# Attention products in column tiles of 32, with x written in its final layout

## The chip, the cores and the metric

The kernel runs on one core of one Trainium2 chip. The metric is the device time of one execution, in microseconds (us); the number quoted for a kernel is the median of its runs. The engines are named as in the profile: PE (TensorE, with its weight loads shown apart as PEld), DVE (VectorE), ACT (ScalarE), POOL (GpSimd), and SP, whose queue issues every transfer (DMA) of this kernel.

## The reference

A gated linear attention with a complex state is followed by a two-layer network with a GELU:

```python
scale = np.minimum(mag, 0.999) / (mag + 1e-06)          # mag = |a_re + i a_im|
for t in range(S):                                       # S = 768
    new_re = ar * S_re - ai * S_im                       # (B, H, D, D) = (4, 8, 48, 48)
    new_im = ar * S_im + ai * S_re
    S_re, S_im = new_re + k[t] v[t]^T, new_im
    y[t] = q[t] . S_re
x = y as (B * S, H * D) = (3072, 384)
out = gelu(x @ w_in) @ w_out                             # w_in 384 x 2048, w_out 2048 x 384
```

The inputs of the attention are float32, the two weight matrices float64.

## The kernel before, in words

**Lanes.** The recurrence over t is turned into a chunked form. The sequence of 768 steps is cut in four groups (GROUPS, line 29: two chunks of 64, two of 64, two of 128, two of 128 steps). For each group, "lanes" of 128 partitions normalise `a`, run a complex running product (`scan`, lines 641 to 654) and multiply k and q by it. A group takes 4, 4, 8 and 8 slices; the last DVE step of a slice writes `xt` (line 631), and three transfers carry it to a scratch tensor `kq` in HBM (lines 633 to 635). This part is nearly all DVE and ACT work.

**Weights.** Each of 32 pieces of 128 x 384 float64 numbers is loaded into one of `N_RAW` buffers `raw`, taken apart by four DVE steps, one ACT copy and three PE products, and kept as a sum of two float32r parts, high and low (`weights`, lines 480 to 506). A buffer can be loaded anew once DVE, ACT and PE have read it.

**Units.** 24 units of 128 rows (one batch, 128 steps) do the attention proper (`unit`, from line 757): load `kqn` from `kq`; transpose k and q of each head on PE into `kT` and `qT`; multiply them to scores (lines 855 to 864); multiply the masked scores, still called `kT` and held in the buffers `kp`, with v into `py` (lines 866 to 873); add the old state `st` times q (`y_state`, lines 875 to 880); and turn and update the state (`turn_by_pe` or `turn_state`, then `add_state`, lines 822 to 839). Units 0 to 3 need the first lane group, units 4 to 7 the second.

In `py`, head h lies in the half h % 2 (64 rows, of which 48 are used) of piece h // 2. So there are four pieces of 96 useful rows, where the network wants three pieces of 128 rows, `xt[:, :, c]`. Pieces 0 to 2 are copied (twice: high part, then low part) straight into `xt`, piece 3 into a helper `x67`, and six transfers of 16 rows each move its rows into the gaps of `xt` (lines 914 to 931). The host lays the rows of w_in out to match (`w_pieces`, lines 222 to 227).

**Blocks.** Nine blocks of two or three units (BLOCKS, line 39) do the network: 16 groups f of 128 columns, for each nine (float32r) products into `ph`, two GELUs on ACT, a subtraction on DVE (`gl`), then nine products into `po` (lines 939 to 983).

**The order.** Every instruction is first noted in a plan; a list scheduler with a table of costs (lines 69 to 98) then chooses engine and order once, when the program is built. On the chip each engine's queue runs in that order and waits where something is late. `MORE` and `BIAS` are numbers that weigh the kinds of work.

All instructions of the plan carry line 398, so rows of the profile are told apart by their tiles: `tile written <- tiles read`.

Of the kernel before, what the change touches and what calls it, by code (L numbers as in the profile page):

```python
# [21 lines left out]
D2 = 2 * D  # L22
# [31 lines left out]
flag_w = flag_x + 2 * NU  # L54
# [28 lines left out]
ENTER, LEAVE = dict(narrow=0.093), dict(narrow=0.1)  # L83
# [8 lines left out]
EARLIER, N_RAW, N_KP = 1, 4, 2  # L92
# [4 lines left out]
MORE = dict(lanes0=70.56, lanes1=16.18, lanes2=-95.71, lanes3=149.81, weights0=-9.95, weights1=-62.12, units0=87.26, units1=95.47, units2=86.78, blocks0=48.05, blocks1=47.29, blocks2=56.39, checks=40.00)  # L97
BIAS = dict(vector=0.45, scalar=-0.52, gpsimd=0.35)
# [11 lines left out]
class Plan:  # L110
# [51 lines left out]
    def add(self, calls):  # L162
# [4 lines left out]
        for call in calls:  # L167
            outs, ins = self.operands(call)
            cost += self.cost(call, outs, ins)
            if engine == "tensor":  # L170
                step.form = ("turn" if call[1] == "transpose" else "round" if call[3]["rhs"].dtype == F32R else
                             "narrow" if call[3]["lhsT"].shape[1] <= 64 else "full")
# [24 lines left out]
    def cost(self, call, outs, ins):  # L197
# [6 lines left out]
        if engine == "tensor":  # L204
# [5 lines left out]

            if cols <= 64:
                return max(0.056, 2 * n * PASS)
# [196 lines left out]
def lanes_and_chunks(ctx, tc, flags, a_lanes, x_lanes, v_units, w_in, w_out, out):  # L409
# [318 lines left out]
    x67s = ring("x67", [128, 2, 128], 1, F32R)  # L728
# [23 lines left out]
    st = [cst.tile([D2, H, D], F32, name=f"st{b}", tag=f"st{b}")[:] for b in range(B)]  # L752
# [4 lines left out]
    def unit(u):  # L757
# [37 lines left out]
        def turn_state(i, b):  # L795

            sb = st[b]
# [9 lines left out]
        def turn_by_pe(i, b):  # L807
# [3 lines left out]
            P.vector.tensor_tensor(out=m2.rearrange("p c (h e) -> p c h e", h=H), in0=vap(sb, [[0, 2], [D, H], [1, D]]),  # L811
# [6 lines left out]
            sf = sb.rearrange("p h e -> p (h e)")  # L818
# [3 lines left out]
        def add_state(chunk, turned):  # L822

            i, _, _, t0, size, b = chunk
            sf = st[b].rearrange("p h e -> p (h e)")
            p = bank()[:, 0:DM] if turned is None else turned
            ps = p[0:D2]
# [37 lines left out]

        def y(some, halves=(0, 1)):

            with P.together():
                for hh in halves:
                    for h in range(hh * 4, hh * 4 + 4):  # L870
                        P.tensor.matmul(out=py[h % 2 * 64:h % 2 * 64 + 64, h // 2], lhsT=vn[:, h], rhs=kT[hh][:, h % 4], start=h < 2,
                                        stop=h > 5 and not with_state)
                y_state(some, halves)

        def y_state(some, halves=(0, 1)):
            for i, _, _, t0, size, b in some:
                for hh in halves:
                    for h in range(hh * 4, hh * 4 + 4):
                        P.tensor.matmul(out=py[h % 2 * 64:h % 2 * 64 + D, h // 2, t0:t0 + size], lhsT=st[b][:, h],
                                        rhs=qT[hh][0:D2, h % 4, t0:t0 + size], start=False, stop=h > 5 and i == with_state[-1][0])  # L880

        if early:
# [5 lines left out]
            py = held[0].rearrange("p (c l) -> p c l", c=4)  # L888
# [7 lines left out]
        else:  # L896
# [4 lines left out]
            py = held[0].rearrange("p (c l) -> p c l", c=4)  # L901
# [12 lines left out]
        xt, x67 = xblk[j][:, u - first_unit[j]], next(x67s)  # L914
        fc = flag_x + 2 * u
        parts = ((py[:, 3], x67[:, 0], x67[:, 1], fc), (py[:, 0:3], xt[:, :, 0], xt[:, :, 1], fc + 1))
        for at, hi, _, f in parts:
            P.scalar.activation(hi, at, AF.Copy, accum_out=flags[:, f:f + 1])
        if u < XPE:
            with P.together():  # L920
                for at, hi, _, _ in parts:
                    P.tensor.matmul(out=at, lhsT=minus[:], rhs=hi, start=False, stop=True, skip_group_check=True)
        for at, hi, lo, _ in parts:
            if u < XPE:
# [329 lines left out]
```

## Time and profile before

| | us |
|---|---|
| median of 3 runs (lowest, highest) | 700.38 (700.11, 700.49) |
| the profiled execution | 697.49 |
| its span, from first to last instruction | 695.8 |
| PE busy | 648.3 |
| DVE busy, ACT busy | 453.6, 465.4 |

The profile is of one execution. "Busy" is the time in which at least one instruction of an engine is under way, and products overlap in it, so a busy PE can still be slow. The granted clock is the share of the full TensorE clock (2.4 GHz) that the chip allowed; 0.5 is the lower level, 1.2 GHz. A float32 product shows as two records, a float32r product as one.

### The profile page before, as it was taken

To read this page: it belongs to the slowest core of one execution; us is meant where nothing else is said; L and a number is where in the kernel's file an instruction comes from. 1 tells how busy PE (TensorE), PEld (TensorE's weight loads), DVE (VectorE), ACT (ScalarE), POOL (GpSimd) and SP (SyncE) were. 2 spreads that over 40 slices of the span, in tenths; PEclk is the share of its full clock that TensorE was granted. 3 is DMA by queue.
4 is the path that set the end of the run, shared out by engine and by line. 5 is a ranking of instruction groups with operands and counts; after the bars stand their busy time and mean duration, and the time that the engine had idled before them with its cause. 6 is when DMAs were issued, how large, how long until landed. Compare 5 with 4: busy or idle time off the path is not lost.

```text
span 695.8 us, 14682 instructions
## 1 busy us (share of the span) xinstructions
PE 648.3 (93%) x5554; PEld 577.4 (83%) x5554; DVE 453.6 (65%) x1135; ACT 465.4 (67%) x1133; POOL 21.7 (3%) x61
## 2 busy tenths in 40 slices
PE   4486897998999999999999999999999999999996
PEld 2142576887899899888999999999999999999995
DVE  7999996997999999999999951244322212112221
ACT  6566676986989988986897764547563653555532
POOL 1001000030000000102000000000000000000000
PEclk9667998999999999999999999999999999999998
DMA  9378775585565557775764654334332523241200
GB/s 280 89 211 237 217 221 173 150 225 180 133 188 128 136 132 193 189 178 155 215 177 116 163 138 134 109 111 124 126 109 75 165 75 93 88 131 47 74 1 27
DMA packets 117325, 99.33 MB, mean 143 GB/s; under 512 B 56192, under 2 KB 105472, under 8 KB 117248
## 3 DMA queue, kind: packets, MB, share of 16 engines
q1 hardware_dynamic: 117248, 98.33, 50.5%
q8 instruction: 45, 0.74, 0.5%
q14 instruction: 32, 0.26, 0.1%
HBM read 69.40 MB, written 23.59 MB: 134 GB/s over the span
## 4 chain that ended last, share of the span: by engine, by line
PE 75%; ACT 8%; DMA 7%; DVE 6%; issue 1%; SPq 1%; ACTq 0%
PE po L398 28%; PE ph L398 26%; PE att L398 20%; DMA kqn<-kq 3%; ACT a L398 2%; DMA kq<-xt 2%; DVE a L398 2%; ACT tab L398 1%; SPq L398 1%; DMA a<-in_w_pieces_dram 1%; DVE tt L398 1%; ACT L396 1%; DVE xt L398 1%; ACT L398 1%; DVE bt L398 1%
## 5 line engine op out<-in xcount | busy, mean ns | idle before, releaser
L398 PE MATMUL ph<-xT,wi_hi 128*128 128x384 f32 (+1 forms) x864 | 209.7, 324 | 3.1 <-DMA xT<-x 3.1
L398 DVE TENSOR_TENSOR gl<-gf,gh 128x384 fp32r<-128x384 f32 (+1 forms) x144 | 73.7, 512 | 160.9 <-ACT gf L398 157.6
L398 PEld LDWEIGHTS ph<-xT,wi_hi 128*128 128x128 f32 x864 | 153.8, 189 | 8.4 <-issue 3.5
L398 ACT ACTIVATE gh<-ph 128x384 fp32r<-128x384 f32 (+1 forms) x144 | 65.5, 455 | 109.8 <-PE ph L398 109.4
L398 PE MATMUL ph<-xT,wi_lo 128*128 128x384 f32 (+1 forms) x432 | 137.8, 319 | 0.0
L398 PE MATMUL po<-wo_hi,gh 128*128 128x384 f32 x384 | 134.7, 351 | 1.4 <-ACT gh L398 1.0
L398 PE MATMUL po<-wo_lo,gh 128*128 128x384 f32 x384 | 128.8, 336 | 0.0
L398 PE MATMUL po<-wo_hi,gl 128*128 128x384 f32 x384 | 92.1, 340 | 0.0
L398 PEld LDWEIGHTS ph<-xT,wi_lo 128*128 128x128 f32 x432 | 81.9, 189 | 0.0
L398 PEld LDWEIGHTS po<-wo_hi,gh 128*128 128x128 f32 x384 | 72.2, 188 | 8.4 <-issue 3.9
L398 PEld LDWEIGHTS po<-wo_lo,gh 128*128 128x128 f32 x384 | 72.4, 189 | 0.1
L398 DVE TENSOR_TENSOR tt<-bt,a 128x192 f32<-128x192 f32 x192 | 67.4, 351 | 0.4
L398 ACT ACTIVATE gf<-ph 128x384 f32<-128x384 f32 (+1 forms) x144 | 65.2, 453 | 2.8 <-DVE gl L398 1.9
L398 PEld LDWEIGHTS po<-wo_hi,gl 128*128 128x128 f32 x384 | 65.2, 188 | 1.5 <-issue 1.1
L398 ACT ACTIVATE a<-a 128x384 f32<-128x384 f32 (+1 forms) x74 | 39.8, 538 | 12.7 <-DMA a<-in_w_pieces_dram 5.4
L398 DVE TENSOR_TENSOR bt<-tt 128x96 f32<-128x96 f32 x192 | 48.0, 250 | 0.3
L398 PE MATMUL att<-qT,kp 96*64 96x64 f32 (+1 forms) x768 | 40.9, 248 | 0.2 <-ACT qT L398 0.2
L398 PEld LDWEIGHTS att<-qT,kp 96*64 96x64 f32 x768 | 35.8, 136 | 5.6 <-ACT qT L398 2.0
L398 DVE TENSOR_TENSOR kp<-att,causal 128x512 f32<-128x512 f32 x48 | 31.8, 685 | 11.9 <-PE att L398 11.9
L398 PE MATMUL po<-raw,ident_r 128*128 128x384 f32 x64 | 32.9, 599 | 7.0 <-ACT wi_lo L398 3.1
L398 PE MATMUL att<-ident_r,kqn 128*96 128x128 f32 x384 | 34.4, 233 | 3.3 <-DMA kqn<-kq 3.3
L398 PEld LDWEIGHTS att<-ident_r,kqn 128*96 128x96 f32 x384 | 32.1, 126 | 6.1 <-DMA kqn<-kq 3.5
(168 smaller groups left out, 973.6 us busy)
## 6 DMA issues: line engine op xcount, KB each, us to landing
kqn<-kq SPq DMA_DIRECT2D x24, 768.0 KB, 5.5
xt<-in_x_lanes_dram SPq DMA_DIRECT2D x24, 384.0 KB, 4.3
kq<-xt SPq DMA_DIRECT2D x24, 384.0 KB, 4.3
kq<-xt SPq DMA_DIRECT2D x48, 192.0 KB, 4.7
a<-in_a_lanes_dram SPq DMA_DIRECT2D x20, 384.0 KB, 3.6
raw<-in_w_pieces_dram SPq DMA_DIRECT2D x16, 384.0 KB, 5.1
raw<-in_moe_w_out_dram SPq DMA_DIRECT2D x16, 384.0 KB, 4.4
vn<-in_v_units_dram SPq DMA_DIRECT2D x24, 256.0 KB, 4.9
```

Of the source, the lines that this page charges most:

```text
L396: self.nc.scalar.preload_act_table_set(table)
L398: getattr(getattr(self.nc, engine), name)(*args, **kw)
```

## The change

1. The products of v and of the state into `py` are made in column tiles of 32 rows instead of 64 or 48: `into` cuts the 48 rows of each head into two windows of 32 columns of its weights, and the 384 rows of x fill three pieces of 128 rows. Of each pair of heads the middle window is shared: 16 rows come from either head, and the zeros of the padding are added to the other's. Twice as many products, half as wide, on four column tiles in turn.
2. `add_state` makes three products of 32 columns for each head instead of two of 64.
3. `x67` and the six transfers for each unit are gone. ACT reads `py` once for the high part (with one sum for the flags instead of two), PE subtracts with one product instead of two in units 0 to 7, and the low part is one copy or subtraction instead of two.
4. The rows of x are in the order of w_in itself, so w_in is loaded directly, in runs of 128 numbers (1 KB) where a row of `w_pieces` had 3 KB.
5. `st` is padded from 48 to 64 columns for each head and cleared by POOL.
6. There are three `raw` buffers instead of four. At the end they also serve as the output buffers.
7. The scheduler's table has a new form "slim" (32 columns) and other values of `MORE` and `BIAS`, which changes the order on all engines.

The diff, cut to its core:

```diff
-EARLIER, N_RAW, N_KP = 1, 4, 2
+EARLIER, N_RAW, N_KP = 1, 3, 2
...
-MORE = dict(lanes0=70.56, lanes1=16.18, lanes2=-95.71, lanes3=149.81, weights0=-9.95, weights1=-62.12, units0=87.26, units1=95.47, units2=86.78, blocks0=48.05, blocks1=47.29, blocks2=56.39, checks=40.00)
+MORE = dict(lanes0=45.21, lanes1=-4.15, lanes2=-65.17, lanes3=158.42, weights0=66.80, weights1=-51.97, units0=90.26, units1=130.91, units2=117.99, blocks0=47.79, blocks1=19.16, blocks2=50.46, checks=97.14)
...
+            if cols <= 32:
+                return max(0.035, n * PASS)
             if cols <= 64:
                 return max(0.056, 2 * n * PASS)
...
-        P.sync.dma_start(out=raw, in_=w_out[f * 128:(f + 1) * 128, :] if o else w_in[f])
+        if o:
+            P.sync.dma_start(out=raw, in_=w_out[f * 128:(f + 1) * 128, :])
+        else:
+            n = raw.shape[1] // NCC
+            P.sync.dma_start(out=raw.rearrange("p (c n) -> p c n", c=NCC), in_=w_in.rearrange("(c p) n -> p c n", p=128)[:, :, f * n:(f + 1) * n])
...
-    st = [cst.tile([D2, H, D], F32, name=f"st{b}", tag=f"st{b}")[:] for b in range(B)]
+    st = [cst.tile([D2, H, 64], F32, name=f"st{b}", tag=f"st{b}")[:] for b in range(B)]
+    for s in st:
+        nc.gpsimd.memset(s, 0.0)
+
+    groups = [[(h * 64, 3 * (h // 2)), (h * 64 + 32, 3 * (h // 2) + 1)] if h % 2 == 0 else
+              [(h * 64 + 16, 3 * (h // 2) + 2), (h * 64 - 16, 3 * (h // 2) + 1)] for h in range(H)]
...
-                    for c0 in (0, 64):
-                        P.tensor.matmul(out=p[c0:c0 + 64, h * D:(h + 1) * D], lhsT=kqn[t0:t0 + size, h].rearrange("p c d -> p (c d)")[:, c0:c0 + 64],
+                    for c0 in (0, 32, 64):
+                        P.tensor.matmul(out=p[c0:c0 + 32, h * D:(h + 1) * D], lhsT=kqn[t0:t0 + size, h, 0, c0:c0 + 32],
...
+        def into(weights, moving, t0, size, halves, final):
+
+            rounds = [[] for _ in range(4)]
+            for k in (0, 1):
+                for h in range(halves[0] * 4, halves[-1] * 4 + 4):
+                    rounds[groups[h][k][1] % 4].append((h,) + groups[h][k])
+            w = weights.rearrange("p h e -> p (h e)")
+            for some in itertools.zip_longest(*rounds):
+                for g, one in enumerate(some):
+                    if one:
+                        h, at, place = one
+                        P.tensor.matmul(out=py[g * 32:(g + 1) * 32, place // 4, t0:t0 + size], lhsT=w[:, at:at + 32], rhs=moving(h),
+                                        start=g not in opened, stop=final and halves[-1] == 1 and one is rounds[g][-1])
+                        opened.add(g)
...
-        parts = ((py[:, 3], x67[:, 0], x67[:, 1], fc), (py[:, 0:3], xt[:, :, 0], xt[:, :, 1], fc + 1))
-        for at, hi, _, f in parts:
-            P.scalar.activation(hi, at, AF.Copy, accum_out=flags[:, f:f + 1])
...
+        hi, lo = xt[:, :, 0], xt[:, :, 1]
+        P.scalar.activation(hi, py, AF.Copy, accum_out=flags[:, flag_x + u:flag_x + u + 1])
...
-        for c in range(NCC):
-            for p0 in (0, 64):
-                P.sync.dma_start(out=xt[p0 + D:p0 + 64, c].bitcast(F32), in_=x67[p0 + c * 16:p0 + c * 16 + 16].bitcast(F32))
```

**The order on PE**, in unit 0 and the start of unit 1, before (`ph`, `po`, `att` are banks of PSUM; `kp` are masked scores; `x2` and so on is the number of like instructions):

```order
L398 MATMUL ph_113<-vn_144,kqn_142 64x48 x16
L398 MATMUL po_114<-kp_149,vn_144 64x128 x4
L398 MATMUL po_114<-qT_147,st_154 48x64 x4
L398 MATMUL ph_112<-m_146,ident_r 128x384
L398 MATMUL ph_112<-m_146,other_half 128x384
L398 MATMUL po_114<-kp_150,vn_144 64x128 x4
L398 MATMUL po_114<-qT_148,st_154 48x64 x4
```

and the same place after:

```order
L400 MATMUL ph_113<-vn_143,kqn_141 32x48 x24
L400 MATMUL po_114<-kp_148,vn_143 32x128 x8
L400 MATMUL po_114<-qT_146,st_152 32x64 x8
L400 MATMUL att_109<-qT_147,kp_149 64x64 x8
L400 MATMUL po_116<-raw_120,ident_r 128x384
L400 MATMUL po_116<-wi_hi,minus 128x384
L400 MATMUL po_116<-wi_lo,minus 128x384
L400 MATMUL ph_112<-m_145,ident_r 128x384
L400 MATMUL ph_112<-m_145,other_half 128x384
L400 MATMUL po_114<-kp_149,vn_143 32x128 x8
L400 MATMUL po_114<-qT_147,st_152 32x64 x8
```

The state's products go from 16 to 24, those into `py` from 4 to 8 for each half of the heads, each 32 wide; the second half's scores and a weight piece stand between the halves now.

**The order on SP**, where the last slices of the second lane group (`kq_106`) are written and the first two units that read it load `kqn`, before (`xT_152<-x_153` are the moves of rows):

```order
L398 DMA kq_106<-xt_135 64x8x96 x2
L398 DMA xT_152<-x_153 16x256 x3
L398 DMA a_128<-in_a_lanes_dram 128x2x384
L398 DMA xT_152<-x_153 16x256 x2
L398 DMA raw_122<-in_w_pieces_dram 128x768
L398 DMA kq_106<-xt_136 64x8x192
L398 DMA kq_106<-xt_136 64x8x96 x2
L398 DMA xT_152<-x_153 16x256
L398 DMA xt_135<-in_x_lanes_dram 128x8x96
L398 DMA kqn_142<-kq_106 128x8x192
```

and after:

```order
L400 DMA kq_106<-xt_134 64x8x96
L400 DMA a_127<-in_a_lanes_dram 128x2x384
L400 DMA kq_106<-xt_135 64x8x192
L400 DMA kq_106<-xt_135 64x8x96 x2
L400 DMA raw_120<-in_moe_w_out_dram 128x768
L400 DMA xt_134<-in_x_lanes_dram 128x8x96
L400 DMA kqn_141<-kq_106 128x8x192
L400 DMA kqn_142<-kq_106 128x8x192
```

Between the last two writes of `kq_106` and ahead of the loads, the moves of rows and a weight load are gone; one weight load stands ahead of the first `kqn` load instead.

**The order on DVE**, at the fourth write of `xt`, the last of the first lane group, with buffer numbers, before:

```order
L398 SCALAR_TENSOR_TENSOR wi_lo_102<-raw2_122,wh_124 128x384
L398 TENSOR_TENSOR a33_128<-a33_128 128x384
L398 TENSOR_TENSOR bt0_129<-tt1_134 128x2x48
L398 SCALAR_TENSOR_TENSOR a33_128<-a33_128 128x384
L398 TENSOR_SCALAR wh_124<-raw3_123 128x384
L398 TENSOR_TENSOR a33_128<-a33_128,xt1_136 128x384
L398 TENSOR_TENSOR a31_126<-att1_110,a31_126 128x384
L398 TENSOR_TENSOR xt1_136<-a33_128,bt1_130 128x8x96
```

and after:

```order
L400 TENSOR_SCALAR wh_123<-raw1_121 128x384
L400 TENSOR_TENSOR a33_127<-a33_127,xt1_135 128x384
L400 SCALAR_TENSOR_TENSOR wo_lo_104<-raw1_121,wh_123 128x384
L400 TENSOR_TENSOR xt1_135<-a33_127,bt1_129 128x8x96
L400 TENSOR_TENSOR a30_124<-a30_124,tab0_130 128x384
L400 TENSOR_SCALAR wh_123<-raw2_122 128x384
```

Before, this write stands behind all four steps of 11 weight pieces and the first step of the twelfth; after, behind all four steps of 14.

## Rows read from the trace of the kernel before

**Rows 1.** The page: in 40 slices of 17.4 us, the busy tenths of PE and of DVE and the granted TensorE clock in tenths.

```profile
PE   4486897998999999999999999999999999999996
DVE  7999996997999999999999951244322212112221
PEclk9667998999999999999999999999999999999998
```

**Rows 2.** Busy time in four stretches that together cover the span up to 688.6 us (us from its start; in this order PE, PEld, DVE, ACT, POOL with the number of records; then the granted clock, the DMA share and GB/s).

```profile
0.00:77.40 77.40, 46.84 (x98) 23.55 (x98) 71.27 (x197) 47.30 (x97) 5.26 (x27) 0.78 0.75 209
77.40:111.70 34.30, 29.23 (x469) 23.21 (x469) 32.42 (x85) 24.50 (x60) 0.00 (x0) 0.98 0.75 215
111.70:158.40 46.70, 43.39 (x359) 38.63 (x359) 37.93 (x97) 38.97 (x85) 6.41 (x12) 0.94 0.65 181
158.40:688.60 530.20, 528.60 (x4628) 491.97 (x4628) 311.82 (x757) 353.86 (x890) 10.04 (x22) 1.00 0.45 126
```

**Rows 3.** What PE waited for, over the whole span: total us, times, longest us.

```profile
PE att L398 <- DMA kqn<-kq: 3.3, 1, 3.3
PE ph L398 <- DMA xT<-x: 3.1, 1, 3.1
```

**Rows 4.** The timeline of PE around its two long waits (start us, us, the instruction, the idle time before it and what ended it), and two windows behind them in the columns of rows 2.

```profile
111.69 0.77 PE L398 MATMUL ph<-xT,wi_hi 128*128 128x256 f32 x2 [3.08 <-DMA xT<-x]
...
158.38 1.09 PE L398 MATMUL att<-ident_r,kqn 128*96 128x128 f32 x8 [3.31 <-DMA kqn<-kq]
...
111.60:117.40 5.80, 5.71 (x22) 5.07 (x23) 3.02 (x9) 3.49 (x8) 0.00 (x0) 0.51 0.33 109
158.40:162.00 3.60, 3.60 (x18) 2.93 (x18) 2.93 (x10) 0.58 (x1) 0.00 (x0) 0.55 1.18 292
```

**Rows 5.** The timeline of SP's queue while rows of x are moved and the second lane group is written out (start us, us for the issues, x their number).

```profile
103.28 6.64 SPq L398 DMA_DIRECT2D xT<-x  x6
...
145.18 0.53 SPq L398 DMA_DIRECT2D raw<-in_w_pieces_dram  x1
145.80 3.14 SPq L398 DMA_DIRECT2D kq<-xt  x3
148.99 1.24 SPq L398 DMA_DIRECT2D xT<-x  x1
...
151.96 0.38 SPq L398 DMA_DIRECT2D kqn<-kq  x1
```

**Rows 6.** The timeline of DVE at the last write of the second lane group, and at its long wait before it.

```profile
118.73 0.43 DVE L398 TENSOR_TENSOR gl<-gf,gh 128x256 fp32r<-128x256 f32 x1 [4.12 <-ACT gf L398]
...
140.21 0.55 DVE L398 SCALAR_TENSOR_TENSOR raw<-raw,wh 128x384 uint32<-128x384 uint32 x1
140.68 0.55 DVE L398 TENSOR_TENSOR a<-a,xt 128x384 f32<-128x384 f32 x1
141.15 0.35 DVE L398 TENSOR_SCALAR wh<-raw 128x384 uint32<-128x384 uint32 x1
141.42 0.95 DVE L398 TENSOR_TENSOR xt<-a,bt 128x768 f32<-128x768 f32 x1
142.29 0.41 DVE L398 TENSOR_TENSOR gl<-gf,gh 128x256 fp32r<-128x256 f32 x1
```

**Rows 7.** Windows between the last write of the first and of the second lane group, in the columns of rows 2.

```profile
66.40:141.40 75.00, 66.50 (x757) 52.80 (x757) 66.64 (x175) 56.22 (x129) 0.15 (x1) 0.93 0.69 197
112.00:121.00 9.00, 9.00 (x59) 8.13 (x60) 4.24 (x12) 6.63 (x16) 0.00 (x0) 0.71 0.41 117
```

**Rows 8.** Transfers of a weight piece (KB each, median us from issue to landing), and SP's waits for PE's products in `po`, most of them for a piece's buffer (total us, times, longest).

```profile
raw<-in_w_pieces_dram SPq DMA_DIRECT2D x16, 384.0 KB, 5.1
raw<-in_moe_w_out_dram SPq DMA_DIRECT2D x16, 384.0 KB, 4.4
...
SPq L398 <- PE po L398: 29.0, 16, 5.3
```

**Rows 9.** The timeline of PE in two later stretches with products of each kind.

```profile
131.10 0.65 PE L398 MATMUL att<-qT,st 96*48 96x64 f32 x16
131.68 0.62 PE L398 MATMUL po<-wo_hi,gl 128*128 128x384 f32 x2
...
301.16 1.14 PE L398 MATMUL att<-vn,kqn 128*64 128x48 f32 x32
302.13 1.06 PE L398 MATMUL att<-kp,vn 128*64 128x128 f32 x16
303.12 0.62 PE L398 MATMUL ph<-xT,wi_hi 128*128 128x384 f32 x2
...
310.97 1.96 PE L398 MATMUL att<-qT,kp 96*64 96x128 f32 x32
312.86 0.45 PE L398 MATMUL po<-wo_hi,gh 128*128 128x384 f32 x1
```

**Rows 10.** Groups over the whole span, by form (busy us, mean ns of one): weight loads of 48 and of 64 columns, and the product that subtracts the high part of `x67`.

```profile
L398 PEld LDWEIGHTS att<-qT,st 96*48 96x48 f32 x416 | 18.3, 122 | 6.8 <-issue 4.8 <-ACT st L398 1.2 <-DVE tt L398 0.2
L398 PEld LDWEIGHTS att<-vn,kqn 128*64 128x64 f32 x384 | 12.2, 138 | 2.8 <-DVE kp L398 1.3 <-issue 1.0 <-DVE gg L398 0.3
L398 PE MATMUL att<-x,minus 128*128 128x128 f32 x6 | 1.5, 254 | 0.0
```

More of the change, by code (lines that the diff above doesn't have):

```diff
@@ L81 @@
 ROUND, PASS = 0.462e-3, 0.4219e-3
-ENTER, LEAVE = dict(narrow=0.093), dict(narrow=0.1)
+ENTER, LEAVE = dict(narrow=0.093, slim=0.093), dict(narrow=0.1, slim=0.1)
 STAY = 1.0
@@ L171, in add @@
                 step.form = ("turn" if call[1] == "transpose" else "round" if call[3]["rhs"].dtype == F32R else
-                             "narrow" if call[3]["lhsT"].shape[1] <= 64 else "full")
+                             "slim" if call[3]["lhsT"].shape[1] <= 32 else "narrow" if call[3]["lhsT"].shape[1] <= 64 else "full")
             if engine == "sync":
@@ L864, in scores @@
                 P.vector.tensor_tensor(out=kT[hh], in0=p.rearrange("p (j l) -> p j l", j=4), in1=vap(masks[chunks[0][4]], [[0, 4], [1, 128]]), op=ALU.mult)
+        opened = set()
+        def into(weights, moving, t0, size, halves, final):
[11 more added lines that the diff above has]
+                        opened.add(g)
         def y(some, halves=(0, 1)):
             with P.together():
[L869 to L872, printed above, removed]
+                into(vn, lambda h: kT[h // 4][:, h % 4], 0, C, halves, not with_state)
                 y_state(some, halves)
@@ L876, in y_state @@
             for i, _, _, t0, size, b in some:
[L877 to L880, printed above, removed]
+                into(st[b], lambda h: qT[h // 4][0:D2, h % 4, t0:t0 + size], t0, size, halves, i == with_state[-1][0])
         if early:
@@ L887, in unit @@
             held.append(bank())
[L888 removed]
+            py = held[0][:, 0:NCC * C].rearrange("p (c l) -> p c l", c=NCC)
             for hh in range(2):
@@ L900, in unit @@
             held.append(bank())
-            py = held[0].rearrange("p (c l) -> p c l", c=4)
+            py = held[0][:, 0:NCC * C].rearrange("p (c l) -> p c l", c=NCC)
             y([])
@@ L913, in unit @@
             xblk[j] = next(xTs)
-        xt, x67 = xblk[j][:, u - first_unit[j]], next(x67s)
-        fc = flag_x + 2 * u
-        parts = ((py[:, 3], x67[:, 0], x67[:, 1], fc), (py[:, 0:3], xt[:, :, 0], xt[:, :, 1], fc + 1))
-        for at, hi, _, f in parts:
-            P.scalar.activation(hi, at, AF.Copy, accum_out=flags[:, f:f + 1])
-        if u < XPE:
[L920 to L924, printed above, removed]
-                P.either(("scalar", "copy", (lo, at), {}), ("vector", "tensor_copy", (lo, at), {}))
-            else:
-                P.vector.tensor_tensor(out=lo, in0=at, in1=hi.bitcast(F32), op=ALU.subtract)
-        for c in range(NCC):
-            for p0 in (0, 64):
-                P.sync.dma_start(out=xt[p0 + D:p0 + 64, c].bitcast(F32), in_=x67[p0 + c * 16:p0 + c * 16 + 16].bitcast(F32))
+        xt = xblk[j][:, u - first_unit[j]]
+        hi, lo = xt[:, :, 0], xt[:, :, 1]
+        P.scalar.activation(hi, py, AF.Copy, accum_out=flags[:, flag_x + u:flag_x + u + 1])
+        if u < XPE:
+            P.tensor.matmul(out=py, lhsT=minus[:], rhs=hi, start=False, stop=True, skip_group_check=True)
+            P.either(("scalar", "copy", (lo, py), {}), ("vector", "tensor_copy", (lo, py), {}))
+        else:
+            P.vector.tensor_tensor(out=lo, in0=py, in1=hi.bitcast(F32), op=ALU.subtract)
     ghs, gls = ring("gh", [128, BLK * C], EARLIER + 1, F32R), ring("gl", [128, BLK * C], EARLIER + 1, F32R)
@@ L1171, in tile_complex_linear_attention_moe @@
         fast.enter_context(tc.manual_schedule())
-        lanes_and_chunks(fast, tc, flags, a_lanes, x_lanes, v_units, w_pieces, w_out, out)
+        lanes_and_chunks(fast, tc, flags, a_lanes, x_lanes, v_units, w_in, w_out, out)
     def within(c0, c1, bound, op):
```

16 lines of the change are left out of this document (8 added, 8 removed).

## Prediction

> **What bounds the kernel now.** I read the page's slices first [rows 1]: PE is full from the tenth slice on, and DVE, nearly full in the first half, is almost idle in the second. The windows [rows 2] make that exact. From 158.4 to 688.6 us PE is busy 528.6 of 530.2 us at a granted clock of 1.00. There only the amount of PE work counts. Before that, PE is busy 46.8 of 77.4 us while the first lane group is computed, 29.2 of 34.3 and 43.4 of 46.7 us. So the time is the moment from which PE is full, plus the PE work left then. Then PE's waits [rows 3] and where they lie [rows 4]: block 0 waits 3.08 us for the moves of x's rows, until 111.69, and the first unit of the second lane group waits 3.31 us for its `kqn`, until 158.38. Behind each wait the granted clock is near the lower level, 1.2 GHz: 0.51 over 5.8 us and 0.55 over 3.6 us, which costs 5.8 x 0.49 = 2.8 and 3.6 x 0.45 = 1.6 us of full-speed work. Last, what sets 158.38. DVE begins the last write of that lane group at 141.42 and begins its next instruction at 142.29 [rows 6]. SP issues the transfers only at 145.80, behind moves of rows and a weight load; `kqn` is asked for at 151.96 [rows 5]. So SP adds 145.8 - 142.4 = 3.4 us, transfers about 13, and the rest is DVE's: busy 66.6 of the 75.0 us since the end of the first lane group, with 4.8 of its 8.4 idle us in one stretch [rows 7], most of it the wait of 4.12 us for the first `gl` [rows 6]. That wait descends from PE's late and slow block 0.
>
> **PE's products.** In `py` and `add_state` two column tiles work at once in the kernel before. Rows show it: a tile that must take eight products of 128 columns alone, in the scores, needs 1.89 us (310.97 to 312.86), while eight shared between two tiles need 0.99 us (302.13 to 303.12) [rows 9]. With 32 columns there are twice the products on four tiles, so each tile has as many as before: four of 128 columns, 0.99 us for a unit, no change if four tiles overlap as two do. `add_state` gives three tiles eight products each, where two tiles had eight: 0.97 us (301.16 to 302.13) again. It can be less: 64-column products of the state take 0.58 us for four on a tile (131.10 to 131.68, the way out of the mode included), 145 ns, and 48-column ones 121 ns, not in proportion to columns, so something else, such as the weight load, has a share. A load takes 138 ns for 64 columns and 122 for 48 [rows 10], 1 ns a column, hence an estimated 106 for 32. If the spacing follows the load, 0.97 becomes 0.97 x 106 / 138 = 0.75 us, -0.22 in each of 28 updates, -6 us. The other side is that tiles don't overlap further: a price for each record, 0.97 us / 32 = 30 ns, whatever its width. Then `add_state` with 48 records costs 1.45 us (+0.48, 28 times, +13.4), and the twelve 64-column state steps, whose records double from 16 to 32, 0.97 instead of about 0.5 us (+0.45 each, +5.4): +19 us. I take a value near the first row, -1 us, because the row with two tiles at work gives half the time of the row with one, so a price for each tile is what the nearest rows show.
>
> PE enters these narrow modes 83 times instead of 81, counted in the order. What a visit adds for its ways in and out is less than the shortest whole phase, 0.58 us [rows 9], so two more add at most 1.2 us; I take +0.5. The product that subtracts the high part of `x67` goes in eight units; 254 ns each with its tail [rows 10], so at most -2, and -0.4 in a full pipeline. PE's sum: about -1 us, bounds -8 and +19.
>
> The Trainium skill (TensorEngine Tiling (Array Packing), Instruction Overhead) says that every product carries an overhead of about 60 cycles and that no tiling factor should be taken from a dimension that is already small. The 48-column rows agree that small products are priced by more than their columns; whether the price is paid per tile or per product no row of two tiles decides. By the rule as a price per product the time is that of the slower rival below.
>
> **The rows that were moved.** 144 transfers go from SP's queue, for six of which the queue was held 6.64 us at 103.28 [rows 5]. In the saturated part that gives nothing, since PE has other work. It gives something twice. Block 0 need no longer wait 3.08 us [rows 3], and the 3.4 us in front of the second lane group's transfers go; a weight load still stands ahead of the first `kqn` load, but behind the writes, where the queue must wait for the landing anyway. Late next is DVE.
>
> **The new order, on DVE.** One weight piece costs DVE two steps of 0.47 us and two of 0.27 us (140.21 to 140.68, 141.15 to 141.42 [rows 6]), 1.48 us. Ahead of the first lane group's last write stand 14 pieces instead of 11 and a quarter: +4.1 us. Of other work, counted step by step with such spacings, 2.1 us less stand there: +2.0. Between that write and the last one of the second group it is 1.1 us less. Together +0.9 us.
>
> **Three raw buffers.** DVE's own work between its last step on a buffer and the first on the next piece in it falls from a median of 14.5 us to 9.6, with 6.3 as the least. What must fit in: PE's release, for which SP waited 29.0 / 16 = 1.8 us on average, and a landing of 4.4 to 5.1 us [rows 8], 6.2 to 6.9 together. w_in's shorter runs move the same bytes. So most reloads arrive in time, a few not: 0 to 6 us, and I take 2, near the lower end.
>
> **Sum.** The second group's arrival at PE: +0.9 (order) + 2.0 (raw) - 5.0 (of 8.4 us of DVE's idle time; the wait for `gl` goes with its cause) - 3.4 (SP) = -5.5 us. PE is not late for it: between the first unit and that point it loses the 3.08 us wait and the 2.8 us of slow clock. In the new order 28 weight pieces instead of 26 stand ahead of it on PE and a few products less, so about 1 us less is left: -1. The slow clock behind the second wait may shrink: -0.5. PE's products: -1, of which -0.5 lie in the full part. Together -7.5 us: 697.5 becomes 690.0 in the profiled execution, which is 2.9 us below the median of the runs; from the median, 700.4 - 7.5 = 692.9 us. Costed at nothing: ACT's one sum fewer for each unit and the one copy fewer on DVE or ACT (both wait for PE later), POOL's four clearings, hidden before the first unit, and three output buffers, since a block writes at most three tiles.
>
> **Rivals.** (a) The ramp gives it back through the raw buffers. If a reload takes 11 us rather than 6.9, the eight reloads ahead of 61 us of DVE work lack 1 to 5 us each, some 6 us in all, and the first unit is late by 8. The arrival then gains nothing: 700 us. For it: DVE is full there, so nothing hides a wait. Against: the waits of SP for PE are short on average.
> (b) Slower: a price per product on PE. It decides as soon as a record in a 32-column group costs as much as one in a 64-column group, 30 ns, and costs 19 us in a stretch where PE has no slack; with the ramp's gain 693 + 19 = 712 us. For it: the 48- and 64-column products are not priced by columns. Against: a tile takes 0.24 us for 128 columns in the scores (1.89 / 8) and 0.145 for 64, so much of the price does follow the tile. If no third and fourth tile ran beside the others at all, the 16 products of a unit would take 1.98 us and the time would pass 740.
> (c) More: the weight load sets the spacing, and `add_state` falls to 0.75 us. 693 - 6 = 687 us.
>
> **How the numbers follow.** The forecast, 693, has a chance of 0.56 and its own range 687 to 698. (a) has 0.17, (b) 0.15 (0.03 of it for the end past 740), (c) 0.12. A measurement of this kernel tells about 0.2%, 1.4 us, from no change. Faster: nearly all of the forecast, (c) and a little of (a), 0.70. Same: half of (a), 0.10. Slower: (b) and the rest of (a), 0.20. The range 684 to 703 takes in (c) and (a) and leaves out (b) and something below.
>
> **What would show it.** Right: PE's wait for `xT` gone; PE full from about 153 instead of 158 us; SP issuing the second group's writes within 1 us of DVE's step; 16 products into `py` in about 1 us and `add_state` at or under 0.97 us. Wrong: DVE waiting for `raw` transfers before 75 us by more than 4 us in all; records of 32 columns 30 ns apart; or PE idle again between 160 and 300 us, where the third lane group could come late for a PE that is ahead.

## The result and the profile after

The changed kernel takes 680.94 us (median of 4 runs, 679.15 to 686.44) beside 700.43 us for the kernel before on the same chip: a ratio of 0.973, with an interval of 0.967 to 0.980. It is 19.5 us faster. The forecast was 7.4 us faster, with a range down to 684 us. The sign was right, and the size was less than half of what came. Here and below, a ratio and its interval leave out executions that count as slow (in e3 one of 1224.61 us, in f2 one of 797.0 us, in e4 four of twelve), so a ratio can differ from the quotient of the two medians.

The profiled execution took 682.73 us, with a span of 681.0. Its slices in the form of [rows 1]:

```profile
PE   4667699999999999999999999999999999999995
DVE  5999989998999999999999954432322221222221
PEclk9777789999999999999999999999999999999999
```

PE is full from about the sixth slice on. The two later dents of the kernel before (slices 7 and 10) are gone, and DVE stays nearly full through them. The windows that answer to [rows 2], cut at PE's first unit, at 108 us and at the first unit of the second lane group:

```profile
0.00:83.60 83.60, 52.51 (x110) 27.29 (x110) 75.75 (x210) 49.95 (x104) 6.75 (x31) 0.82 0.72 210
83.60:108.00 24.40, 24.28 (x448) 19.26 (x451) 21.00 (x56) 17.56 (x39) 0.00 (x0) 0.86 0.56 178
108.00:155.00 47.00, 45.97 (x631) 39.47 (x621) 45.77 (x119) 40.52 (x88) 4.24 (x12) 1.00 0.81 218
155.00:673.40 518.40, 517.65 (x5648) 484.07 (x5648) 308.31 (x737) 344.39 (x812) 6.90 (x22) 1.00 0.47 125
```

The last stretch, in which only the amount of PE work counts, is 518.4 us long instead of 530.2. It begins at 155.0 instead of 158.4 us. So of the 14.8 us by which the two profiled spans differ, 11.8 lie in the part that I had called full and 3.4 ahead of it; the tail behind it is 0.4 us longer.

PE's waits, as in [rows 3]:

```profile
PE att L400 <- DMA kqn<-kq: 3.1, 2, 2.1
```

The wait for `xT` is gone. What is left for `kqn` is 2.06 us at the very first unit and 1.09 us in front of the second lane group's first unit, at 155.06. The second lane group's last write, on DVE and then in SP's queue, against [rows 5, 6]:

```profile
139.27 0.95 DVE L400 TENSOR_TENSOR xt<-a,bt 128x768 f32<-128x768 f32 x1
140.14 0.55 DVE L400 SCALAR_TENSOR_TENSOR wi_lo<-raw,wh 128x384 fp32r<-128x384 uint32 x1
```

```profile
141.17 3.78 SPq L400 DMA_DIRECT2D kq<-xt  x3
145.12 0.65 SPq L400 DMA_DIRECT2D raw<-in_moe_w_out_dram  x1
145.81 1.06 SPq L400 DMA_DIRECT2D xt<-in_x_lanes_dram  x1
148.73 1.00 SPq L400 DMA_DIRECT2D kqn<-kq  x2
```

SP issues the writes 1.0 us behind DVE's step (141.17 against 140.14), where it was 3.4 us, and asks for `kqn` at 148.73 instead of 151.96.

PE's products of each kind, against [rows 9]; the columns after the tiles are rows x columns of the weights, then the moving data, then the number of records:

```profile
305.76 0.84 PE L400 MATMUL att<-vn,kqn 128*32 128x48 f32 x45
306.40 0.30 PE L400 MATMUL att<-kp,vn 128*32 128x128 f32 x1
306.43 0.22 PE L400 MATMUL att<-vn,kqn 128*32 128x48 f32 x3
306.47 1.05 PE L400 MATMUL att<-kp,vn 128*32 128x128 f32 x31
...
318.80 1.08 PE L400 MATMUL att<-kp,vn 128*32 128x128 f32 x32
319.81 0.44 PE L400 MATMUL po<-wo_hi,gh 128*128 128x384 f32 x1
...
321.91 0.88 PE L400 MATMUL att<-vn,kqn 128*32 128x48 f32 x48
322.72 0.79 PE L400 MATMUL po<-wo_hi,gl 128*128 128x384 f32 x3
```

Sixteen products of 32 columns into `py` take 1.01 us (318.80 to 319.81), where eight of 64 took 0.99. Four column tiles overlap as fully as two. But `add_state` takes 0.71 us where it stands next to other products of 32 columns (305.76 to 306.47) and 0.81 us between full products (321.91 to 322.72). The 0.97 us of [rows 9] stood next to products of 64 columns. Between full products a visit had taken 1.07 us (331.78 to 332.85, kernel before):

```profile
331.78 1.14 PE L398 MATMUL att<-vn,kqn 128*64 128x48 f32 x32
332.85 0.75 PE L398 MATMUL att<-ident_r,kqn 128*96 128x128 f32 x8
```

So with like neighbours the visit is 0.26 us cheaper in both places. From start to next start over all records of the trace, its 28 visits fall from 28.88 to 22.49 us, -6.4 us, of which -5.6 lie in the last stretch.

The same sums over the last stretch give the rest of its 11.8 us: -3.1 for weight pieces (8 records of raw products are left in it instead of 12, with the products that go with them), -2.4 for the products into `po`, some of which had run at the slow clock behind 158.4 us [rows 4], -0.9 of idle time and -1.1 of smaller terms, against +1.3 for six more records into `ph`.

### The profile page after: what moved, and what is told of

Read it like the earlier page. It is cut to its first block, busy times and chain, and to the rows that moved or that the text cites. A ratio compares the mean times of both kernels' runs of the same rounds, so it can differ in the third digit from the quotient of the medians.

```text
span 681.0 us, 16837 instructions
## 1 busy us (share of the span) xinstructions
PE 640.7 (94%) x6826; PEld 570.2 (84%) x6826; DVE 451.0 (66%) x1120; ACT 453.2 (67%) x1041; POOL 17.9 (3%) x65
## 4 chain that ended last, share of the span: by engine, by line
PE 74%; DVE 13%; DMA 5%; ACT 3%; issue 3%; SPq 1%; DVEq 0%
PE po L400 29%; PE ph L400 27%; PE att L400 19%; DVE a L400 3%; DVE tt L400 2%; DVE xt L400 2%; DMA kqn<-kq 2%; DVE bt L400 2%; DMA xt<-in_x_lanes_dram 1%; DVE wh L400 1%; DMA kq<-xt 1%; ACT a L400 1%; DVE tab L400 1%; DVE raw L400 1%; DMA a<-in_a_lanes_dram 1%
## 5 line engine op out<-in xcount | busy, mean ns | idle before, releaser
L400 PE MATMUL po<-wo_hi,gh 128*128 128x384 f32 x384 | 133.2, 347 | 0.1
L400 PE MATMUL po<-raw,ident_r 128*128 128x384 f32 x64 | 34.3, 623 | 13.9 <-ACT wi_lo L400 6.1
L400 ACT ACTIVATE a<-a 128x384 f32<-128x384 f32 (+1 forms) x77 | 41.5, 540 | 7.0 <-DMA a<-in_moe_w_in_dram 2.7
```

Of the source, the lines that this page charges most:

```text
L400: getattr(getattr(self.nc, engine), name)(*args, **kw)
```

## The experiments

Each result stands beside runs of the kernel before on the same chip at the same time: 698.85 us (median) for the runs that begin with e, 698.2 with f, 699.1 with g, 699.9 with h. The four groups ran on four chips, so a comparison across groups goes by the ratios. The changed kernel's executions differ by some 7 us, those of the kernel before by up to 16 (f), and the medians of the kernel before by 2, so I call nothing under 2 us shown.

**The changed kernel again.** 

> The changed kernel itself, as the mark for the runs beside it. If its 2.7% is a property of the program and not of one session, the ratio lies at 0.970 to 0.977 again. If a part of it was luck of the granted clock in the first 110 us, it comes nearer to 0.98, the 14.8 us by which the two profiled spans differ.

680.73 us (677.47 to 684.57), ratio 0.974 (0.969 to 0.979). Its profiled execution, 677.47 us, is faster than the first one, and the trace tells where (windows in the columns of [rows 2], first of the changed kernel's first profile, then of this one):

```profile
75.00:95.00 20.00, 17.12 (x234) 11.81 (x234) 17.27 (x49) 13.61 (x30) 0.00 (x0) 0.77 0.70 216
```

```profile
75.00:95.00 20.00, 17.12 (x292) 11.81 (x290) 19.36 (x53) 13.92 (x30) 0.00 (x0) 1.00 0.82 257
149.80:668.00 518.20, 517.61 (x5648) 484.03 (x5648) 308.53 (x737) 345.14 (x813) 7.52 (x24) 1.00 0.47 125
```

In these 20 us around the first unit PE is busy for 17.12 us in both. In one execution the granted clock is 0.77, in the other 1.00, and 234 records get done instead of 292. The second lane group's first unit then runs at 149.8 instead of 155.1 us. But the clock isn't all of it. The two executions are apart before that stretch: at DVE's very first wait for a load, and so at the first unit (each time the first profile, then this one):

```profile
8.72 0.36 DVE L400 TENSOR_SCALAR wh<-raw 128x384 uint32<-128x384 uint32 x1 [3.04 <-DMA raw<-in_moe_w_in_dram]
6.93 0.36 DVE L400 TENSOR_SCALAR wh<-raw 128x384 uint32<-128x384 uint32 x1 [1.22 <-DMA raw<-in_moe_w_in_dram]
```

```profile
83.68 0.93 PE L400 MATMUL att<-ident_r,kqn 128*96 128x128 f32 x8 [2.06 <-DMA kqn<-kq]
80.70 0.76 PE L400 MATMUL att<-ident_r,kqn 128*96 128x128 f32 x8 [1.73 <-DMA kqn<-kq]
```

Of the 5.2 us between the two arrivals, 3.0 are there at the first unit, 1.8 of them already behind that first load; 2.3 come behind it, where the slow clock lies. The last stretch has the same length in both, 518.2 and 518.4 us. So the front of this kernel varies by 5 us from one execution to the next, by the first load and by the clock, and the full part doesn't.

**The narrow state products alone.** In the changed kernel, with order and everything else held; the edit in effect:

```diff
-                    for c0 in (0, 32, 64):
-                        P.tensor.matmul(out=p[c0:c0 + 32, ...], lhsT=kqn[t0:t0 + size, h, 0, c0:c0 + 32], ...)
+                    for c0 in (0, 64):
+                        P.tensor.matmul(out=p[c0:c0 + 64, ...], lhsT=kqn[t0:t0 + size, h]...[:, c0:c0 + 64], ...)
```

> The changed kernel with one thing undone: add_state makes two products of 64 columns for each head again, and the order of everything else is held (the scheduler is shown the three products, the two are issued). Theory A (the three narrow products are cheaper, 0.80 instead of 1.03 us for an update, and PE has no slack): 6 us slower than the changed kernel, 1.0% of the time. Rival (the saving only moves waits, or is made up by the gelu and copies that follow): under 2 us.

688.99 us (686.56 to 689.61), ratio 0.985 (0.980 to 0.989): 8.3 us slower than the changed kernel. `add_state` and the last stretch, in this kernel:

```profile
321.43 1.14 PE L406 MATMUL att<-vn,kqn 128*64 128x48 f32 x32
322.50 0.80 PE L406 MATMUL po<-wo_hi,gl 128*128 128x384 f32 x3
```

```profile
151.70:677.20 525.50, 524.44 (x5329) 490.21 (x5328) 310.24 (x741) 345.73 (x813) 6.17 (x22) 1.00 0.47 124
```

A visit takes 1.07 us (321.43 to 322.50), and the last stretch 525.5 us, 7.3 more than in e1. Here it takes 1.07 us also next to products of 32 columns, where the kernel before had 0.97 next to those of its own width:

```profile
304.89 1.14 PE L406 MATMUL att<-vn,kqn 128*64 128x48 f32 x32
305.96 1.08 PE L406 MATMUL att<-kp,vn 128*32 128x128 f32 x32
```

So the narrow state products are worth 7 to 8 us in this kernel, a little more than the 6.4 us against the kernel before, and they are the largest single part of the gain that the forecast lacked.

**The same in the order of before**, an edit that leaves every instruction but the products of `add_state` where it was. 

> The kernel before with one thing changed: add_state makes three products of 32 columns for each head; order held. Theory A: 6 us faster than the kernel before, ratio 0.991, nearly all of it in the part where PE is full. Rival (the saving needs the new order, which was made for the shorter step): under 2 us, ratio 0.997 or more.

699.45 us (690.05 to 703.72), ratio 0.997 (0.992 to 1.001). No gain shows, against the expected 6 us. That this order's waits in front hide it is a guess; the next runs take these waits away.

**The moves of rows.** First added to the changed kernel: six transfers of 16 rows each, issued by SP behind each unit's x into a scratch tensor that nothing reads.

```diff
+            for kw in s.behind:
+                self.nc.sync.dma_start(**kw)
...
+        P.steps[-1].behind = [dict(out=moved[p0 + D:p0 + 64, c], in_=xt[p0 + c * 16:p0 + c * 16 + 16, c].bitcast(F32)) for c in range(NCC) for p0 in (0, 64)]
```

> The changed kernel with six transfers of 16 rows added behind each unit's x, on SP's queue at the place where the low part is done, and nobody waiting for them; order held. Theory A (the queue was held by the moves, and that delayed the second lane group): SP issues the second group's writes later by 1 to 3 us, and the kernel is slower by 1 to 3 us. Rival (only the wait of block 0 for the rows cost time, the queue has room): under 1 us.

701.85 us (697.31 to 706.35, and one execution of 1224.61), ratio 1.003 (1.000 to 1.007): 21 us slower than the changed kernel, where 1 to 3 us were expected, and far more than the issues themselves take. Unlike in the kernel before, these moves have no place of their own in the plan: each stands right behind the step that makes its data. SP's waits, and ACT's waits for its transfers, in this kernel:

```profile
SPq L402 <- DVE xT L400: 89.6, 10, 35.4
```

```profile
ACT tab L400 <- DMA a<-in_a_lanes_dram: 12.3, 7, 3.4
ACT a L400 <- DMA a<-in_moe_w_in_dram: 11.9, 7, 3.4
ACT a L400 <- DMA a<-in_moe_w_out_dram: 10.6, 5, 6.6
```

And the same three of ACT in e1:

```profile
ACT tab L400 <- DMA a<-in_a_lanes_dram: 2.3, 4, 1.2
ACT a L400 <- DMA a<-in_moe_w_in_dram: 2.6, 2, 2.1
ACT a L400 <- DMA a<-in_moe_w_out_dram: 1.6, 1, 1.6
```

SP stands for 89.6 us in front of moves whose x isn't ready, and the loads behind them in the queue are late. ACT waits 34.8 us for its three kinds of loads where it had waited 6.5. In the end PE waits too, also where it had been full (e3, then e1):

```profile
160.00:692.00 532.00, 520.12 (x5626) 485.41 (x5625) 306.21 (x730) 341.52 (x806) 7.02 (x22) 0.99 0.46 122
```

```profile
150.00:668.00 518.00, 517.42 (x5648) 483.85 (x5647) 308.33 (x737) 344.94 (x813) 7.32 (x23) 1.00 0.47 125
```

11.9 us of idle PE (532.0 - 520.12) against 0.6; 9.5 of them lie between 160 and 450 us. The longest wait of SP, 35.4 us from 578 us on, meets a PE without idle time (50.00 of 50 us busy from 550 to 600): a held queue costs by what stands behind it then.

Then taken out of the kernel before: the moves are planned, so that the order holds, and not issued; POOL clears the `xt` buffers instead.

```diff
+                if engine == "sync" and "x67" in kw["in_"].tensor.name:
+                    continue
```

> The kernel before, in its own order on every engine, without the 144 transfers that move rows of x (they are planned, so that nothing else moves, but not issued; the rows that they would fill stay zero, so block products are made on an x of which a quarter is left out). Theory Q (the moves cost by holding SP's in-order queue, everywhere and not only at the two waits that I counted): 10 to 16 us faster than the kernel before, about 686 us, and PE's idle time falls by 8 us or more. Rival N (the moves cost what I counted, 3.4 us of queue and a wait of 3.08 us, and the rest of the gain is the new order's numbers): 3 to 6 us faster, about 695 us.

687.95 us (686.40 to 689.38), ratio 0.985 (0.980 to 0.990): 10.2 us faster, as theory Q had it, though PE's idle time falls by 6 us (47.5 to 41.5) and not by 8. The second lane group's first unit runs at 152.7 instead of 158.4 us, and the last stretch is 2.4 us shorter than that of [rows 2]:

```profile
152.70:680.50 527.80, 526.48 (x4629) 490.72 (x4628) 312.19 (x761) 357.18 (x894) 10.07 (x22) 1.00 0.44 123
```

Last, the queue against the traffic: the same transfers in POOL's queue, first in e3's kernel, then in the whole kernel before, with the blocks still waiting for their rows.

```diff
-                self.nc.sync.dma_start(**kw)
+                self.nc.gpsimd.dma_start(**kw)
```

> The kernel of e3_after_moves (the changed kernel with six transfers of 16 KB behind each unit's x that nothing waits for) with these transfers in POOL's queue instead of SP's. The same bytes move at nearly the same times, but SP's queue isn't held. Theory Q (what costs is SP's in-order queue, held by a transfer whose data isn't there yet): most of the 21 us that they cost on SP is gone, 681 to 686 us. Rival T (the transfers themselves cost, by their traffic or their ports): about 700 us as on SP.

> The kernel before, whole, with its 144 moves of rows in POOL's queue instead of SP's, in its own order on PE, DVE and ACT. The blocks still wait for the moved rows. Theory Q: most of the 10 us that leaving the moves out gives (f1_before_nomoves) comes from the queue alone, so 688 to 692 us; what is left above 688 is the wait of block 0. Rival T: 697 us or more, or slower where POOL's issues are slow.

g1: 685.95 us (681.99 to 689.00), ratio 0.979 (0.973 to 0.986); g2: 691.13 us (689.16 to 697.43), ratio 0.989 (0.982 to 0.996). So of the 21 us that the moves cost on SP about 5 stay (4 by the ratios), and in the kernel before a change of queue alone brings about 8 of the 10 us that leaving the moves out brings. What the rest is stays open. POOL's queue in g1:

```profile
POOL moved L402 <- DVE xT L400: 211.2, 10, 44.6
POOL moved L402 <- ACT xT L400: 140.4, 8, 33.5
```

POOL stands 351.6 us in front of moves, some four times as long as SP, and it hurts little: next to nothing is behind them there. Most of the price was the holding of SP's in-order queue, not the 144 transfers.

**Both parts in the order of before.** 

> As the run above (no moves issued, rows of x left out), and add_state in three products of 32 columns for each head, still in the order of the kernel before. Theory Q: 6 to 8 us faster than the run above, since PE is no longer held up by late loads: about 679 to 681 us, all of the gain of the changed kernel without its order. Rival N: the step is 6 us too, but from a higher level, about 688 us. If narrow products gain little in the order of before for a reason of their own, the step is 0 to 2 us.

687.91 us (685.61 to 691.07, and one execution of 797.0), ratio 0.984 (0.979 to 0.990): no step against f1, where theory Q expected 6 to 8 us. The trace splits it in two (f1, then f2):

```profile
85.00:105.00 20.00, 20.00 (x298) 15.76 (x294) 18.55 (x47) 15.38 (x39) 0.00 (x0) 1.00 0.71 212
```

```profile
85.00:105.00 20.00, 20.00 (x234) 15.14 (x225) 12.04 (x29) 9.84 (x24) 0.00 (x0) 0.63 0.42 122
158.00:682.70 524.70, 523.22 (x4950) 486.12 (x4948) 312.17 (x762) 356.42 (x894) 10.05 (x22) 1.00 0.44 124
```

The last stretch is 3.1 us shorter than f1's (524.7 against 527.8), `add_state` saving 4.1 in it. That is less than in the changed kernel: the products into `py` are 64 wide here, and a narrow visit next to them takes 0.81 us (0.97 when it was 64 wide), where it takes 0.71 among products of 32. But the last stretch begins 5.3 us later, behind one in which PE was busy all the time at a granted clock of 0.63, where f1 had 1.00. Were the narrow products in the first units to blame? Three kernels keep these wide (g3 and h1 here, h3 further down); the edit in effect:

```diff
-                    for c0 in (0, 32, 64): ...
+                    for c0 in (0, 64) if i < 2 else (0, 32, 64): ...
```

> As f2_before_nomoves_state32 (moves not issued, so rows of x left out), but the narrow products of add_state only from the second lane group on; the first four units keep the products of 64 columns. Theory C (in f2 the narrow products saved 4 us in the full part and lost as much in the ramp, where the granted clock lay at 0.50 to 0.77 for 30 us): with the first units as in f1_before_nomoves the saving shows, about 684 us. Rival O (the saving doesn't reach the end in that order for another reason): 688 us, as f1 and f2.

> The changed kernel with add_state of the first four units in products of 64 columns as before, of 32 columns from the fifth unit on; order held. Theory C (narrow state products in the ramp make the granted clock fall more often behind the first unit): the eight wide visits cost 1.5 to 2 us more of PE where PE isn't the limit, and the slow stretch between 80 and 95 us goes, so the median is 677 to 680 us and the spread small, some 3 us as with e2_after_state64. Rival S (the slow stretch comes by chance and not from the narrow products): 681 to 683 us with the spread of the changed kernel, some 7 us.

> The changed kernel once more, beside h1_after_late on the same chip: 679 to 682 us by both theories, with a spread of some 7 us.

g3: 686.09 us (685.52 to 691.82), ratio 0.983 (0.977 to 0.990), its last stretch 524.8 us and beginning at 152.1: between both theories. h1: 686.06 us (681.35 to 687.60), ratio 0.981 (0.977 to 0.986); h2: 681.21 us (679.70 to 682.62), ratio 0.975 (0.971 to 0.979). Theory C falls: with wide products in front the changed kernel is 4.9 us slower, not faster, and the slow stretch is there with them (h1, then h2). Rival S, with 681 to 683 us, missed h1 too.

```profile
80.00:95.00 15.00, 13.85 (x195) 10.99 (x195) 12.64 (x32) 9.75 (x21) 0.00 (x0) 0.77 0.58 172
```

```profile
80.00:95.00 15.00, 12.84 (x264) 9.56 (x266) 14.44 (x38) 10.50 (x23) 0.00 (x0) 1.00 0.71 221
```

So the slow stretch behind the first unit isn't brought by narrow products. It comes in some executions and not in others, and what decides it stays open. That the eight wide visits cost 4.9 us by the medians, when they take 2.6 us more of PE, stays open too. For e2 it matters little: in its profile 7.3 us lie in the last stretch, behind these eight.

**The order.** The numbers MORE and BIAS, exchanged between the two kernels. 

> The kernel before with the changed kernel's MORE and BIAS alone, so with another order on every engine and everything else as it was, the moves among it. Theory Q: the numbers are worth little by themselves, within 4 us of the kernel before, to either side. Rival N: 6 us faster or more, about 692 us.

> The changed kernel with MORE and BIAS of the kernel before, so all of its products and no moves, in an order weighed by the old numbers. Theory Q: it keeps most of the gain, 680 to 686 us. Rival N: it loses 6 us or more against the changed kernel, 688 us or above.

f3: 725.17 us (721.77 to 728.01), ratio 1.040 (1.034 to 1.045). f4: 704.34 us (701.86 to 712.07), ratio 1.010 (1.006 to 1.014). f3 is against both theories; f4 lies where rival N had it, 688 us or above, and against theory Q. Either kernel loses some 25 us with the other's numbers (27.0 by f3; f4 by its ratio, 1.010 against 0.974). In f4, the stretch below shows PE idle for 7.8 us just behind the second lane group's first unit and runs at 0.86, since the next unit comes late: its transposes begin at 194.8 us, in e1 at 171.8.

```profile
152.70:200.00 47.30, 39.51 (x382) 29.93 (x383) 43.88 (x115) 34.42 (x69) 0.00 (x0) 0.86 0.53 156
```

Numbers that suit the program are thus needed for the gain; they aren't a gain that could be had without the rest.

**A version with another order.** The planner's table gives a transfer 2.2 us of latency, while the loads of the changed kernel land after 3.7 to 6.2 us (medians by kind).

```diff
-FETCH = 2.2
+FETCH = 4.0
...
-MORE = dict(lanes0=45.21, lanes1=-4.15, lanes2=-65.17, ...
+MORE = dict(lanes0=54.19, lanes1=-105.94, lanes2=-615.33, ...
```

> The changed kernel in another order: the planner's table takes 4.0 us for a transfer's latency in place of 2.2, near the 3.8 to 6.3 us that the profile shows, with numbers MORE and BIAS that suit this. If orders lose on the chip because transfers land later than planned (as the moves on SP's queue do), it is faster than the changed kernel: 672 to 678 us. If the changed kernel's order is already limited by PE's work alone from the second lane group on, no change: 679 to 683 us. A worse fit on DVE would make it slower than 684 us.

> The order of g4_after_latency4 with the wide state products in the first four units. Theory C: 677 to 679 us and little spread. Rival S: 680 to 682 us, the wide products' price on top of g4.

g4: 679.45 us (677.44 to 680.84), ratio 0.971 (0.965 to 0.976); h3: 680.80 us (679.27 to 688.31), ratio 0.976 (0.970 to 0.981). g4 is the lowest median of all, 1 to 2 us below the changed kernel, which these runs can't tell from no change, and h3, with wide products in front, is 1.4 above g4 (on another chip), no more than noise. The order that came with the change was good enough; PE is busy for 517.65 of the 518.40 us of its last stretch.

## Why the prediction was wrong in size, point by point

**What bounds the kernel.** Right. The time is the moment from which PE is full plus the PE work left, and both terms moved. I put that moment at about 153 us; it was 155.0 in the first profile and 149.8 in e1.

**PE's products.** This is the step that failed: "I take a value near the first row, -1 us". The row with two tiles showed that tiles overlap, and this held (1.01 us for `py`). But I carried the 0.97 us of `add_state` over to the narrower tile as if a tile's price didn't know its width. It measured 0.71 to 0.81 us, -6.4 us in the trace and 8.3 us between e2 and e1. That is the price of rival (c), 0.75 us at a chance of 0.12, though its 687 us was still too slow. Nor was 0.97 the price of all 28 visits: their mean was 28.88 / 28 = 1.03 us, since a visit that isn't next to products of its own shape costs more. The reason given for rival (c) was the weight load, estimated at 106 ns; the trace has 107 ns as the median (it was 138 at 64 columns [rows 10]):

```profile
L400 PEld LDWEIGHTS att<-vn,kqn x1152: 102/107/110, 110.9 to 490.8; 64*32 64x32 f32 x96, 128*32 128x32 f32 x96
```

The ratio of the loads, 107 / 138 = 0.78, and that of the columns, 3 x 32 / (2 x 64) = 0.75, are too near to each other for these runs to say which of the two sets the spacing.

The Trainium skill (TensorEngine Tiling (Array Packing), Instruction Overhead) gives every product an overhead and says not to take a tiling factor from a dimension that is already small. Read as a price per product on whatever tile, as I did, it fails here: 48 records took less time than 32 had, 17 ns each (0.81 / 48) instead of 33 (1.07 / 32), both between full products. Read as a price on each tile it isn't contradicted, since a tile had 16 records before and has 16 after. Rival (b), which rested on the first reading, is out by that.

**The rows that were moved.** Mostly right, and for the right reason. The queue's 3.4 us fell to 1.0, PE's wait went, and taken alone these moves cost 10.2 us (f1), where the sum of the terms that I gave them was 5.0 + 3.4 + 0.5 = 8.9. That the two sums are near is in part luck: in f1's profile the arrival comes 5.7 us earlier, not 8.4 (DVE is 3.1 us late there already at the first lane group's last write, 68.6 against 65.5), and 2.4 us come from the last stretch. The term of 5.0 held: between the two groups' last writes DVE's idle time fell from 8.4 us [rows 7] to 4.3 in the first profile, 2.3 in e1 and 3.2 in f1, and its wait of 4.12 us for `gl` is 0.49 in e1. Wrong was the sentence that the moves give nothing in the saturated part: there they gave those 2.4 us in the kernel before, and 11.9 us of idle PE in e3. One row of the trace of before, which I had not read, points at it:

```profile
SPq L398 <- DVE x L398: 41.4, 12, 19.8
```

SP had stood 41.4 us in front of moves of rows. The longest wait, 19.8 us, ends only at 648 us, but nearly all of the others lie between 250 and 585 us.

**The new order and the raw buffers.** I charged +0.9 for the order and +2.0 for three buffers. Little of it came. DVE's last write of the second lane group begins at 139.27, just the 2.1 us earlier that the terms add up to (+0.9 + 2.0 - 5.0). That is luck: this execution lost time on the first load and had the slow clock behind the first unit. In e1 and h2 the write begins at 134.9 and 135.4. There the first lane group's last write comes 0.6 and 1.0 us later than before (66.1 and 66.5 against 65.5), where order and buffers were to add up to 4.0. DVE's waits for w_in's pieces:

```profile
DVE wh L400 <- DMA raw<-in_moe_w_in_dram: 5.2, 2, 3.0
```

Of the 5.2 us 3.04 are its very first wait, for the first load of all, and 2.1 come at 156 us, behind the arrival. Between them none shows. So rival (a) is out; its own sum was wrong too, since eight reloads that lack 1 to 5 us each lack 8 us at least, not 6. The first load waits in the kernel before as well (0.86 us in its profile, 2.31 in f1's), so it isn't the buffers' price. With everything but the narrow state products, e2 stands at 688.99, where f1 stands at 687.95 with the moves alone gone: the new order, three buffers, w_in's short runs and four tiles in `py` together moved about 1 us (both ratios are 0.985), which is not to be told from none. What each of these did alone, no run shows.

**Work left for PE.** I counted 28 weight pieces instead of 26 ahead of the second lane group and took -1, and -0.5 for the slow clock behind the second wait. The trace shows -3.1 us of products of weight pieces in the last stretch, and a share of the -2.4 us in `po`. Same sign, a third of the size.

**The sum.** Of the 12 us that the forecast lacked, some 6 are the state's narrow products (6.4 by the trace and 8.3 by e2, less the 1 us that the forecast had), some 3 the charges for order and buffers that weren't paid, and the rest small terms of the right sign. This split is an estimate, not a measurement of each term. The two parts that were taken alone, the moves (10.2 in f1) and the state's products (8.3 in e2), make 18.5 of the 19.5 us, though in two different orders. The profiled execution, with its late first load and its slow stretch, shows only 14.8 us.

## What to carry to other kernels

A price measured on one tile width is not a price per tile: here it went nearly with the columns (or with the weight load's duration), so scale it before it is carried over, compare visits that have like neighbours, and fill the array where a matrix has fewer columns than the tiles take, as here the 96 columns of the state's products, which had been loaded as 128. In `py`, where each tile has as many products as before, narrower tiles brought no time. A transfer that waits for data in an in-order queue costs what stands behind it, so read that queue's own waits first, also in stretches where the transfers' bytes are hidden; a queue with nothing behind costs little. A table of priorities belongs to one program: judge a change with numbers that suit it, since the old ones can turn a gain of 19 us into a loss of 6, as in f4. And two profiles of the same program can differ by 5 us in the front: look where they part before a cause is named.

## What the runs showed of the hardware that I had not expected

The front differs from one execution to the next of the same program. PE's granted clock around the first unit was 0.77 in one and 1.00 in the other at the same busy time (17.12 of 20 us), and some 2 us came behind the first unit with it; DVE's wait for its first load was 3.04 us in one and 1.22 in the other. A change of tile width costs about 0.1 us a visit, as much as a change from full products: `add_state` in products of 64 columns takes 0.92 and 0.97 us next to products of its own width in the kernel before, and 1.07 next to full products or, in e2, next to products of 32 columns; in products of 32 it takes 0.71 next to its own and 0.81 next to full products or, in f2, to products of 64.
